# Reordering a slot on TensorE: the output product between the gate and the val matmuls

## The chip, the cores and the metric

The kernel runs on one core of one Trainium2 chip. The metric is the device time of one execution in microseconds. The input tensors lie in device memory as float32, and the output goes back as float32. The engines are named here as the profile names them: PE is TensorE's matmul, PEld its weight load, DVE is VectorE, ACT is ScalarE, POOL is GpSimd and SP is SyncE.

## The reference

Four batches of 6016 rows with 256 channels go through a cross-covariance attention, and the result goes through a gated feed-forward layer.

```python
def _attn_ref(q, k, v, tau):
    qn = q / (np.linalg.norm(q, axis=1, keepdims=True) + 1e-06)
    kn = k / (np.linalg.norm(k, axis=1, keepdims=True) + 1e-06)
    s = kn.transpose(0, 2, 1) @ qn / tau          # 256 x 256 per batch
    s = s - s.max(-1, keepdims=True)
    a = np.exp(s)
    a /= a.sum(-1, keepdims=True) + 1e-09
    return (v @ a).astype(np.float32)

def _moe_ref(x, w_gate, w_val, w_out):            # x: 24064 x 256, d_ff = 1536
    gate = 1.0 / (1.0 + np.exp(-(x @ w_gate)))
    val = x @ w_val
    return (gate * val @ w_out).astype(np.float32)
```

The scores `s` need a sum over all rows of a batch before that batch's feed-forward part can begin. The kernel folds the attention matrix into the weights: `G = a @ w_gate` and `H = a @ w_val`, so that `x @ w_gate` becomes `v @ G`. The sigmoid is written as a tanh: `sigmoid(z) * val` is half of `(tanh(z/2) + 1) * val`, and the half is carried by the constant 2 in the softmax's sums.

## The kernel before

The feed-forward part of batch `b` is cut into 12 chunks of 512 rows (the twelfth has 384), and each chunk into 12 **slots**, one for each block `f` of 128 of the 1536 hidden features. 4 x 12 x 12 makes 576 slots. A slot has these parts:

- **gate** and **val**: two matmuls of 512 columns each, into `ps_gate` and `ps_val`. Each of these PSUM pools has two buffers, so val of slot f needs the buffer that val of slot f-2 had.
- **tanh** on ACT, from `ps_gate` to `g_sb`.
- the **gating step** on DVE, `(tanh + 1) * val`, which writes block `f` of `hT` and frees `ps_val`.
- a **share of the output product** of the chunk before: 7 matmuls of 128 columns out of 84, into `ps_o`.
- **side work** for the next batch: scores on PE, squares on ACT, sums on DVE, additions and transfers on POOL.

```python
    psg = pool("psg", 2, space=PSUM)
    psv = pool("psv", 2, space=PSUM)
    pso = pool("pso", 2, space=PSUM)
    ...
    def glu(b, ci, f, between=None):
        ...
        ps_gate = psg.tile([P, CH], FP32, tag="g", name="ps_gate")
        ps_val = psv.tile([P, CH], FP32, tag="v", name="ps_val")
        for ps, w in ((ps_gate, G), (ps_val, H)):
            for ib in range(CB):                       # CB = 2
                mm(ps[:, :n], w[...][:, ib, ...], vT[:, ib, :nt, :], start=(ib == 0), stop=(ib == CB - 1))
            if between is not None and w is G:
                between()
        g_sb = gpool.tile([P, CH], FP32, tag="g", name="g_sb")
        nc.scalar.activation(out=g_sb[:, :n], in_=ps_gate[:, :n], func=ACT.Tanh, scale=0.5)
        nc.vector.scalar_tensor_tensor(
            out=hts[b, ci][:, f, :n], in0=g_sb[:, :n], scalar=1.0, in1=ps_val[:, :n],
            op0=ALU.add, op1=ALU.mult,
        )
```

The output product multiplies 2 x 2 blocks by a scheme with seven products in place of eight. Two of the seven (y1 and x1) take blocks of `hT` as they are; the other five (z1, x2, y2, z2, v2) take **sums** of two blocks, which DVE forms in `a_sum`. One `a_sum` forms one of the five sums for one half `g` of the hidden features. For half 0 this happens while the chunk itself is worked on, for half 1 in the first slots of the chunk after it.

```python
PRODUCTS = {  # name: (region of ps_o, left operand, right operand); a bare number is a sum
    "z1": (0, 1, 3), "y1": (1, (0, 0), 1), "x1": (2, (1, 1), 0), "x2": (2, 3, (0, 0)),
    "y2": (1, 2, (1, 1)), "z2": (0, 0, 2), "v2": (3, 4, 4),
}
ORDER = (
    (0, "y1"), (1, "y1"), (0, "x1"), (0, "z1"), (1, "x1"), (1, "z1"),
    (0, "x2"), (0, "y2"), (0, "z2"), (0, "v2"),
    (1, "x2"), (1, "y2"), (1, "z2"), (1, "v2"),
)
NEXT_SLOTS = {1: 1, 3: 3, 4: 2, 5: 0, 6: 4}        # slot: which sum, half 1, of the chunk before
OWN_SLOTS = {7: 1, 8: 3, 9: 2, 10: 0, 11: 4}       # slot: which sum, half 0, of this chunk
    ...
    def run_work(work, share):                         # take this share of the list, run it
        upto = sum(w[0] for w in work) * share
        done = 0
        while work and done < upto:
            cost, fn, *args = work.pop(0)
            fn(*args)
            done += cost
    ...
    for b in range(B):
        side = side_work(b)
        for ci in range(NCH):
            final = (b, ci) == (B - 1, NCH - 1)
            for f in range(FC):
                mid = gh_mid.get(f) if (b, ci) == (0, 0) else None
                glu(b, ci, f, None if mid is None else (lambda: gh_pieces(mid)))
                if prev is not None:
                    if f == 4:
                        store()
                    if f + final in NEXT_SLOTS and prev != (0, 0):
                        a_sum(*prev, 1, NEXT_SLOTS[f + final])
                    run_work(work, 1 / max(1, FC - final - f))
                if f in OWN_SLOTS and not final and (b, ci) != (0, 0):
                    a_sum(b, ci, 0, OWN_SLOTS[f])
                for fn, a in spill.get((b, ci, f), []) + side.get((ci, f), []):
                    fn(*a)
```

Every product runs over six indices `i`; `i` 0 to 2 uses half 0 of a sum and `i` 3 to 5 half 1. When the product z1 or v2 of a half of the rows ends, ACT copies a part of the bank (z1) or all of it (v2) out of `ps_o`, POOL adds the copies together, and SP stores the rows. A chunk of 384 rows has 42 of the small matmuls and 12 of 256 columns. All engines work through their instructions in the order of this program.

Of the kernel before, what the change touches and what calls it, by code (L numbers as in the profile page):

```python
# [9 lines left out]
FP32 = mybir.dt.float32  # L10
BF16 = mybir.dt.bfloat16
INT32 = mybir.dt.int32
ACT = mybir.ActivationFunctionType
# [40 lines left out]
def kernel(  # L54
# [20 lines left out]
    nc = tc.nc  # L75
    P = nc.NUM_PARTITIONS
# [9 lines left out]
    FC = DFF // P  # L86
# [3 lines left out]
    CH = TPC * P  # L90
# [11 lines left out]
    def pool(name, bufs, **kw):  # L102
        return ctx.enter_context(tc.tile_pool(name=name, bufs=bufs, **kw))
# [10 lines left out]
    gpool = pool("gpool", 3)  # L114
# [13 lines left out]
    def mm(out, lhsT, rhs, start, stop, **kw):  # L128
        nc.tensor.matmul(out, lhsT=lhsT, rhs=rhs, start=start, stop=stop, **kw)  # L129
# [74 lines left out]
    for f0, nf in pieces:  # L204
        if f0 + nf == DFF:
            load_v(0, 1)
        for w, src in enumerate((moe_w_gate, moe_w_val)):
            nc.gpsimd.dma_start(
                out=w_sb[w][f0 // FG][:, :, ds(f0 % FG, nf)],
                in_=src.rearrange("(t p) f -> p t f", p=P)[:, :, ds(f0, nf)],  # L210
# [5 lines left out]
    for n in range(FC // TPC):  # L216
        w_f32[n] = f32pool.tile([P, TPC, C], FP32, tag="f32", name="w_f32")
        nc.gpsimd.dma_start(
            out=w_f32[n], in_=moe_w_out.rearrange("(t p) c -> p t c", p=P)[:, n * TPC : (n + 1) * TPC, :]
# [413 lines left out]
    def gh(b, piece, pl, tag, act=None):  # L633
        gh_store(b, piece, gh_mms(b, piece, pl, tag), piece[3] == 0 if act is None else act)
# [25 lines left out]
    def glu(b, ci, f, between=None):  # L660
        t0, nt = groups[ci]
        n = nt * P
        G, H = st[b]["gh"]
        vT = vts[b, ci]
        if f == 0:
            hts[b, ci] = hpool.tile([P, FC, CH], BF16, tag="hT", name="hT")
        ps_gate = psg.tile([P, CH], FP32, tag="g", name="ps_gate")
        ps_val = psv.tile([P, CH], FP32, tag="v", name="ps_val")
        for ps, w in ((ps_gate, G), (ps_val, H)):
            for ib in range(CB):  # L670
                mm(
                    ps[:, :n],
                    w[f // (FG // P)][:, ib, ds(f % (FG // P) * P, P)],
                    vT[:, ib, :nt, :],
                    start=(ib == 0),
                    stop=(ib == CB - 1),
                )
            if between is not None and w is G:
                between()
        g_sb = gpool.tile([P, CH], FP32, tag="g", name="g_sb")  # L680
        nc.scalar.activation(out=g_sb[:, :n], in_=ps_gate[:, :n], func=ACT.Tanh, scale=0.5)  # L681
        nc.vector.scalar_tensor_tensor(  # L682
            out=hts[b, ci][:, f, :n],
            in0=g_sb[:, :n],
            scalar=1.0,
            in1=ps_val[:, :n],
            op0=ALU.add,
            op1=ALU.mult,
        )
# [3 lines left out]
    def a_sum(b, ci, g, m):  # L693

        nt = groups[ci][1]
        half = nt // 2
        hT = hts[b, ci]
        if (b, ci, g) not in sums:
            sums[b, ci, g] = spool.tile(
                [P, len(A_SUMS), FC // 4, CH // 2], BF16, tag=f"s{g}", name="sums", bufs=2 - g  # L700
            )
        (r0, k0), op, (r1, k1) = A_SUMS[m]
        f0, f1 = g * (FC // 2), (g + 1) * (FC // 2)
        nc.vector.tensor_tensor(  # L704
            out=sums[b, ci, g][:, m, :, : half * P],
            in0=hT[:, f0 + k0 : f1 : 2, ds(r0 * half * P, half * P)],
            in1=hT[:, f0 + k1 : f1 : 2, ds(r1 * half * P, half * P)],
            op=op,
        )
# [94 lines left out]
    def run_work(work, share):  # L804
# [8 lines that stand above are left out]
    def store():  # L813
        while stores:
            b, ci = stores.pop(0)
            t0, nt = groups[ci]
            nc.sync.dma_start(out=out_rows[b][:, t0 : t0 + nt, :], in_=ffn.pop((b, ci))[:, :nt, :])
# [43 lines left out]
    for g, (t0, nt) in enumerate(groups0):  # L861
# [11 lines left out]
        while adds:  # L873
            w, last_sq = adds.pop()
# [157 lines left out]
    def gh_pieces(ns):  # L1032
        for n in ns:
            gh(0, gh_first[n], *gh_banks[n % 4])

    prev = None
# [3 lines that stand above are left out]
            final = (b, ci) == (B - 1, NCH - 1)  # L1040
            for f in range(FC):
                mid = gh_mid.get(f) if (b, ci) == (0, 0) else None
                glu(b, ci, f, None if mid is None else (lambda: gh_pieces(mid)))
                if prev is not None:
                    if f == 4:
                        store()
                    if f + final in NEXT_SLOTS and prev != (0, 0):
                        a_sum(*prev, 1, NEXT_SLOTS[f + final])
                    run_work(work, 1 / max(1, FC - final - f))
                if f in OWN_SLOTS and not final and (b, ci) != (0, 0):  # L1050
                    a_sum(b, ci, 0, OWN_SLOTS[f])
                for fn, a in spill.get((b, ci, f), []) + side.get((ci, f), []):
                    fn(*a)
                if (b, ci) == (0, 0):
                    gh_pieces(gh_end.get(f, ()))
            prev = (b, ci)
            if not final:
                work = out_work(*prev)
# [39 lines left out]
```

## Time and profile before

| What | Value |
|---|---|
| median of 3 runs | 803.82 us (802.44 to 803.94) |
| span of the profiled execution | 799.6 us |
| granted TensorE clock, mean | 0.998 |
| PE busy | 779.7 us, 6875 matmuls |
| PEld busy | 497.6 us |
| DVE busy | 713.9 us |
| ACT busy | 525.6 us |
| POOL busy | 398.9 us |
| 576 gating steps on DVE | 385.3 us busy, 670 ns each on average |
| 576 tanh on ACT | 337.9 us busy, 589 ns each on average |
| 460 `a_sum` on DVE | 283.4 us busy, 616 ns each on average |

The page gives, for each engine, the time in which at least one of its instructions was under way. Rows of the costliest groups read: line, engine, operation, written tile <- read tiles, shape, count, then busy time and mean duration, then the idle time of that engine just before these instructions and what ended most of it. The timeline gives start, duration and the instruction. Matmuls overlap: one of 512 columns is shown with 0.38 us, but the next one starts 0.216 us after it. So the distance from start to start tells PE's rate.

### The profile page before, as it was taken

To read this page: it belongs to the slowest core of one execution; us is meant where nothing else is said; L and a number is where in the kernel's file an instruction comes from. 1 tells how busy PE (TensorE), PEld (TensorE's weight loads), DVE (VectorE), ACT (ScalarE), POOL (GpSimd) and SP (SyncE) were. 2 spreads that over 40 slices of the span, in tenths; PEclk is the share of its full clock that TensorE was granted. 3 is DMA by queue.
4 is the path that set the end of the run, shared out by engine and by line. 5 is a ranking of instruction groups with operands and counts; after the bars stand their busy time and mean duration, and the time that the engine had idled before them with its cause. 6 is when DMAs were issued, how large, how long until landed. Compare 5 with 4: busy or idle time off the path is not lost.

```text
span 799.6 us, 18217 instructions
## 1 busy us (share of the span) xinstructions
PE 779.7 (98%) x6875; PEld 497.6 (62%) x6875; DVE 713.9 (89%) x1228; ACT 525.6 (66%) x891; POOL 398.9 (50%) x618
## 2 busy tenths in 40 slices
PE   3899999999999999999999999999999999999998
PEld 2556666666666666666666666666666566666666
DVE  5768999999979999999988999999998898998996
ACT  3666777766667767676667777666666565665664
POOL 3564545446453566565743565565744244444433
PEclk9999999999999999999999999999999999999999
DMA  9997758432777899862577699977234323423302
GB/s 214 198 199 133 131 96 139 93 67 54 135 143 140 170 174 200 171 114 54 115 137 146 132 163 186 174 147 139 56 66 84 67 56 80 74 60 72 82 27 74
DMA packets 82776, 95.16 MB, mean 119 GB/s; under 512 B 52512, under 2 KB 58528, under 8 KB 82688
## 3 DMA queue, kind: packets, MB, share of 16 engines
q0 software_dynamic: 25616, 55.85, 39.5%
q1 hardware_dynamic: 56496, 37.30, 21.2%
q8 instruction: 53, 0.87, 0.4%
q10 hardware_dynamic: 576, 0.85, 0.3%
q14 instruction: 35, 0.29, 0.1%
HBM read 79.04 MB, written 24.64 MB: 130 GB/s over the span
## 4 chain that ended last, share of the span: by engine, by line
PE 94%; DMA 4%; DVE 1%; issue 0%; ACT 0%; POOL 0%; DVEq 0%; POOLq 0%
PE ps_gate L129 30%; PE ps_val L129 30%; PE ps_o L129 27%; DMA qk_sb<-in_k_dram 4%; PE ps_s L129 4%; PE ps_gh L129 3%; DVE hT L682 0%; DVE sums L704 0%; DVE qs L364 0%; PE ps_end L129 0%; PE ps_n L129 0%; DVE x_sb L543 0%; PE ps_r L129 0%; ACT e_sb L561 0%; POOL qk_sb L148 0%
## 5 line engine op out<-in xcount | busy, mean ns | idle before, releaser
L681 ACT ACTIVATE g_sb<-ps_gate 128x512 f32<-128x512 f32 (+1 forms) x576 | 337.9, 589 | 224.7 <-PE ps_gate L129 212.3
L682 DVE SCALAR_TENSOR_TENSOR hT<-g_sb,ps_val 128x512 bf16<-128x512 f32 (+1 forms) x576 | 385.3, 670 | 67.1 <-ACT g_sb L681 52.3
L129 PE MATMUL ps_val<-vT,gh_H 128*128 128x512 bf16 (+1 forms) x1152 | 337.5, 375 | 0.5 <-DVE hT L682 0.5
L129 PE MATMUL ps_gate<-vT,gh_G 128*128 128x512 bf16 (+1 forms) x1152 | 337.6, 375 | 0.0
L704 DVE TENSOR_TENSOR sums<-hT 128x768 bf16<-128x768 bf16 (+1 forms) x460 | 283.4, 616 | 0.0
L129 PEld LDWEIGHTS <-sums 128*128 128x128 bf16 x2670 | 182.9, 98 | 82.2 <-DVE sums L704 0.4
L129 PEld LDWEIGHTS <-gh_H 128*128 128x128 bf16 x1152 | 112.7, 98 | 131.5 <-issue 1.2
L775 POOL TENSOR_TENSOR out_sb<-out_sb,m_sb 128x256 f32<-128x256 f32 x89 | 78.8, 885 | 186.1 <-ACT out_sb L765 163.0
L129 PE MATMUL ps_o<-w_sums,sums 128*128 128x128 bf16 x1602 | 154.4, 219 | 0.0
L129 PEld LDWEIGHTS <-hT 128*128 128x128 bf16 x1200 | 88.3, 98 | 46.8
L759 POOL TENSOR_TENSOR m_sb<-m_sb 128x128 f32<-128x128 f32 x89 | 44.9, 504 | 127.1 <-ACT m_sb L758 126.7
L129 PEld LDWEIGHTS <-gh_G 128*128 128x128 bf16 x1152 | 92.5, 98 | 12.2 <-DVE gh_G L629 0.3
L129 PE MATMUL ps_o<-w_out_sb,sums 128*128 128x128 bf16 x1068 | 96.2, 219 | 0.0
L129 PE MATMUL ps_o<-w_sums,hT 128*128 128x128 bf16 x1068 | 95.5, 219 | 0.0
L776 POOL TENSOR_TENSOR out_sb<-out_sb 128x256 f32<-128x256 f32 x89 | 76.6, 861 | 7.0
L760 POOL TENSOR_TENSOR m_sb<-m_sb 128x128 f32<-128x128 f32 x89 | 56.6, 636 | 7.0
L765 ACT COPY out_sb<-ps_o 128x512 f32<-128x512 f32 x89 | 52.2, 586 | 11.4 <-PE ps_o L129 8.9
L129 PE MATMUL ps_s<-qk_sb 128*128 128x256 bf16 (+1 forms) x194 | 34.1, 292 | 15.7 <-DMA qk_sb<-in_k_dram 8.6
L758 ACT COPY m_sb<-ps_o 128x384 f32<-128x384 f32 x89 | 42.6, 479 | 3.7 <-PE ps_o L129 1.1
L257 ACT ACTIVATE sq<-qk_sb 128x1024 bf16<-128x1024 bf16 (+3 forms) x36 | 35.6, 1009 | 12.0 <-DMA qk_sb<-in_k_dram 11.9
L297 ACT ACTIVATE sq<-qk_sb 128x1024 bf16<-128x1024 bf16 (+1 forms) x40 | 41.2, 1031 | 0.0
L129 PEld LDWEIGHTS <-qk_sb 128*128 128x128 bf16 x286 | 26.7, 102 | 21.7 <-issue 10.9
(102 smaller groups left out, 448.0 us busy)
## 6 DMA issues: line engine op xcount, KB each, us to landing
out_dram<-out_sb SPq DMA_DIRECT2D x43, 512.0 KB, 3.4
v_sb<-in_v_dram POOLq DMA_DIRECT2D x44, 256.0 KB, 5.4
acc<-sq POOLq DMA_DIRECT2D x16, 512.0 KB, 7.0
qk_sb<-in_q_dram POOLq DMA_DIRECT2D x14, 512.0 KB, 10.3
qk_sb<-in_k_dram POOLq DMA_DIRECT2D x14, 512.0 KB, 8.2
qs<-qk_sb POOLq DMA_DIRECT2D x20, 256.0 KB, 5.5
qk_sb<-in_q_dram POOLq DMA_DIRECT2D x15, 256.0 KB, 4.6
qk_sb<-in_k_dram POOLq DMA_DIRECT2D x15, 256.0 KB, 5.6
```

The costliest lines, as they stand in the source:

```text
L129: nc.tensor.matmul(out, lhsT=lhsT, rhs=rhs, start=start, stop=stop, **kw)
L257: nc.scalar.activation(out=sq[:, :nt, :], in_=src[:, :nt, :], func=ACT.Square)
L297: nc.scalar.activation(out=s["sq", w][:, u0 : u0 + n, :], in_=src[:, u0 : u0 + n, :], func=ACT.Square)
L681: nc.scalar.activation(out=g_sb[:, :n], in_=ps_gate[:, :n], func=ACT.Tanh, scale=0.5)
L682: nc.vector.scalar_tensor_tensor(out=hts[b, ci][:, f, :n], in0=g_sb[:, :n], scalar=1.0, in1=ps_val[:, :n], op0=ALU.add, op1=ALU.mult,)
L704: nc.vector.tensor_tensor(out=sums[b, ci, g][:, m, :, : half * P], in0=hT[:, f0 + k0 : f1 : 2, ds(r0 * half * P, half * P)], in1=hT[:, f0 ...
L758: nc.scalar.copy(m, states[p]["ps"][:, : 3 * P].rearrange("p (n c) -> p n c", c=P))
L759: nc.gpsimd.tensor_tensor(out=m[:, 1, :], in0=m[:, 1, :], in1=m[:, 2, :], op=ALU.add)
L760: nc.gpsimd.tensor_tensor(out=m[:, 2, :], in0=m[:, 1, :], in1=m[:, 0, :], op=ALU.add)
L765: nc.scalar.copy(o[:, p : p + half + 1 : half, :], states[p]["ps"].rearrange("p (t c) -> p t c", c=C),)
L775: add(out=ends, in0=ends, in1=states[p]["m"][:, 1:3, :], op=ALU.add)
L776: add(out=ends, in0=ends, in1=mids, op=ALU.subtract)
```

## The change: where the output product stands in a slot

The change moves each slot's share of the output product from behind val to between gate and val. `glu` has a hook for this, `between`, which the first chunk already used for other matmuls. The tanh is now issued right after the gate matmuls, ahead of the hook, so that in ACT's order it stays ahead of the copies of `ps_o` that the output product may call for. The aim is that tanh runs while PE is at the output product, so that it is done by the time val is.

```diff
         ps_gate = psg.tile([P, CH], FP32, tag="g", name="ps_gate")
         ps_val = psv.tile([P, CH], FP32, tag="v", name="ps_val")
+        g_sb = gpool.tile([P, CH], FP32, tag="g", name="g_sb")
         for ps, w in ((ps_gate, G), (ps_val, H)):
             for ib in range(CB):
                 mm(
@@
-            if between is not None and w is G:
-                between()
-        g_sb = gpool.tile([P, CH], FP32, tag="g", name="g_sb")
-        nc.scalar.activation(out=g_sb[:, :n], in_=ps_gate[:, :n], func=ACT.Tanh, scale=0.5)
+            if w is G:
+                nc.scalar.activation(out=g_sb[:, :n], in_=ps_gate[:, :n], func=ACT.Tanh, scale=0.5)
+                if between is not None:
+                    between()
         nc.vector.scalar_tensor_tensor(
@@
                 mid = gh_mid.get(f) if (b, ci) == (0, 0) else None
-                glu(b, ci, f, None if mid is None else (lambda: gh_pieces(mid)))
+                if prev is not None:
+                    mid = lambda: run_work(work, 1 / max(1, FC - final - f))
+                elif mid is not None:
+                    mid = lambda ns=mid: gh_pieces(ns)
+                glu(b, ci, f, mid)
                 if prev is not None:
                     if f == 4:
                         store()
                     if f + final in NEXT_SLOTS and prev != (0, 0):
                         a_sum(*prev, 1, NEXT_SLOTS[f + final])
-                    run_work(work, 1 / max(1, FC - final - f))
```

No instruction is added or taken away. In a slot PE had gate, val, output, scores; it now has gate, output, val, scores. DVE's order is as before: gating step, `a_sum`, side work. In ACT's order only the first chunk differs, where tanh now stands ahead of the copies that build G and H.

## The prediction

> **What bounds the kernel now.** I began with the page's busy times and its chain of waits.
>
> ```profile
> PE 779.7 (98%) x6875; PEld 497.6 (62%) x6875; DVE 713.9 (89%) x1228; ACT 525.6 (66%) x891; POOL 398.9 (50%) x618
> PE 94%; DMA 4%; DVE 1%; issue 0%; ACT 0%; POOL 0%; DVEq 0%; POOLq 0%
> ```
>
> PE holds 94% of the chain that ended last, and the 4% of DMA is the head, where the first q and k arrive. DVE is second and close. A busy share of 98% doesn't prove that PE runs at its rate, so I went on to the timeline of PE in a middle slot.
>
> ```profile
> 495.78 0.59 PE L129 MATMUL ps_gate<-vT,gh_G 128*128 128x512 bf16 x2
> 496.21 0.59 PE L129 MATMUL ps_val<-vT,gh_H 128*128 128x512 bf16 x2
> 496.64 0.55 PE L129 MATMUL ps_o<-w_sums,sums 128*128 128x128 bf16 x7
> 497.03 0.28 PE L129 MATMUL ps_s<-qs,qk_sb 128*128 128x128 bf16 x2
> 497.14 0.59 PE L129 MATMUL ps_gate<-vT,gh_G 128*128 128x512 bf16 x2
> ```
>
> From start to start, gate takes 0.43 us, val 0.43, seven output matmuls 0.39, two scores 0.11: 1.36 us together. That is 4 x 0.216 + 9 x 0.056. I took the same distances over the whole trace: the medians are 216 ns behind a matmul of 512 columns and 56 ns behind one of 128. After 60 us, the distances that exceed their kind's value by over 60 ns add up to only **1.1 us** of excess: 0.78 us ahead of two val groups, 0.25 us ahead of one score and 0.09 us elsewhere. So PE runs back to back for 740 us. It waits for nobody.
>
> Then the waits, and the two costliest groups:
>
> ```profile
> DVE hT L682 <- ACT g_sb L681: 52.3, 117, 1.3
> PE ps_val L129 <- DVE hT L682: 0.5, 2, 0.3
> PEld L129 <- DVE sums L704: 0.4, 1, 0.4
> L681 ACT ACTIVATE g_sb<-ps_gate 128x512 f32<-128x512 f32 (+1 forms) x576 | 337.9, 589 | 224.7 <-PE ps_gate L129 212.3
> L682 DVE SCALAR_TENSOR_TENSOR hT<-g_sb,ps_val 128x512 bf16<-128x512 f32 (+1 forms) x576 | 385.3, 670 | 67.1 <-ACT g_sb L681 52.3
> ```
>
> The 52.3 us in which DVE waits for tanh are what the change aims at. But that is idle time of an engine that isn't the bound. PE's own waits for DVE, the second and third line, come to 0.9 us.
>
> [...] this trace shows 56 in such streams[...], and output matmuls have no slack from weight loads that another order could win back. [...] loads of sums begin about 0.2 us ahead of their matmuls. So a late sum holds up all that PE has behind it, val included. [...] The `a_sum` rows fit that: 550 ns in the median, 1809 ns at most, with POOL additions beside the long ones. The rows don't prove the cause.
>
> **The change, part by part.**
>
> *Removed:* nothing on PE. The same 6875 matmuls are issued at the same rate. What can vanish is PE's wait ahead of val for its PSUM buffer, 0.78 us. Val comes 0.39 us later in its slot (7 x 56 ns), while the gating step that frees its buffer moves by at most about 0.25 us (next paragraph), so this wait gets more room. The most that can be won is the whole 1.1 us, **0.1%**.
>
> *Moved, DVE:* before, the gating step could start 1.26 us after the slot's gate at the earliest (minimum over the trace, 1.39 in the median): 0.43 for gate, about 0.2 until tanh starts, 0.6 tanh. After, tanh is done at that same 1.23 to 1.26, but val ends its issue at 0.43 + 0.39 + 0.43 = 1.25, and with the same 0.2 us of latency the step starts at 1.45 to 1.46. So steps that used to start before 1.46 come later, by 0.2 us at most; later ones, where DVE was behind, don't move. Over all steps of 512 columns the mean move is 0.09 us. DVE's wait for tanh turns into a wait for val of about the same length. It doesn't become shorter: DVE's work and PE's period stay as they are.
>
> *Moved, the output product:* relative to its slot's gate it stands **0.43 us earlier** (val's two matmuls), while the sums come no earlier and in part up to 0.2 us later. This is the cost. From the order of the program I paired each of the 3822 output matmuls in the loop with the sum or gating step that it needs, and took the room between that operation's end and the matmul's start. The median is over 8 us. The tight ones are all the first use of half 1 of a sum, `i` = 3: z1 in slot 3 (or slot 2 for 384 rows), y2, z2 and v2 in slots 6 to 8. For chunks of 512 rows, z1 has 1.01 us in the median and 0.06 at the least. One is already late, at 475 us:
>
> ```profile
> 473.53 1.42 DVE L704 TENSOR_TENSOR sums<-hT 128x768 bf16<-128x768 bf16 x1
> 474.48 0.59 PE L129 MATMUL ps_val<-vT,gh_H 128*128 128x512 bf16 x2
> 474.99 0.17 PEld L129 LDWEIGHTS <-sums 128*128 128x128 bf16 x3 [0.42 <-DVE sums L704]
> 475.00 0.34 PE L129 MATMUL ps_o<-w_sums,sums 128*128 128x128 bf16 x3
> ```
>
> The sum ended at 474.95, and val had filled the time up to 474.91. With the output product ahead of val, PE would stand still from 474.48 to 474.99. That one slot costs 0.4 to 0.5 us.
>
> *The sum:* a matmul that had to wait still shows 0.06 us of room, so a slot becomes late where its smallest room is under 0.43 + 0.06 = 0.49 us. Within a chunk I count only the largest shortfall, because PE's delay gives room to the next slots too. That makes **13 chunks and 2.4 us**. With the full extra delay of the gating step (a threshold of 0.65) it is 18 chunks and 4.9 us; with 0.55 it is 14 and 3.3. Tight slots are mostly those in which DVE was behind, whose sums don't move, so I stay near the low end: +2.5 us. Less the 0.8 us ahead of val this is **+1.7 us**, and 803.8 + 1.7 = **805.5 us**.
>
> *Off the path:* ACT's copies of `ps_o` are asked for 0.43 us sooner relative to gate. Before, a copy at a slot's end delayed the next tanh; after, it ends while val runs. A tanh that starts late because of a square (1.05 us) has 0.82 us of output and val to hide in. POOL's additions follow the copies, and their waits (163.0 us behind the copies in one row of the page) are idle time of a half-empty engine. In the first chunk tanh goes ahead of the copies that build G and H, with a few tenths of a microsecond either way.
>
> **The rivals.**
>
> *Tanh was the hidden bound, so the change wins several per cent.* For it: 52.3 us of DVE waits for tanh, and DVE busy 89%, 92% between 60 and 780 us (662.66 of 720). Against it: DVE's lateness reaches PE in only about 1 us of 740. Were it true, PE's starts would show gaps; they don't. It would make 765 to 785 us. I hold it for all but excluded.
>
> *PE becomes bound to DVE's sums in most chunks.* For it: the median room of the z1 sum is only 1.01 us, and up to 0.63 of that goes; DVE has only 8% of spare time, so a backlog drains slowly. Were every one of 46 product chunks to lose 0.4 us, that is +18 us, and 822 us. Against it: nine tenths of the z1 rooms are over 0.72 us, still enough after the shift.
>
> *Nothing happens at all.* The rooms shift with how POOL and DVE happen to meet, and a wait of PE gives DVE time to catch up, so the late slots could cost under 1 us and cancel what val no longer waits. It would make 803 to 804.
>
> **Range and chances.** The runs of before spread over 1.5 us. The lower end is no late sum, no wait ahead of val and a low draw: 802.5. The upper end is twice the larger estimate of the late sums, 2 x 2.4 to 4.9 us, less a little: 809.5. A 2% gain needs 787.7 us, which is below what 6875 matmuls at their rate permit: 0.5%. A 2% loss needs 819.9 us, almost the second rival in full: 2.5%. Between lies 97%.
>
> **What would show it.** In the profile after: PE busy and matmul count nearly unchanged; DVE's wait for tanh small, and in its place a wait of the gating step for val, some tens of microseconds; PE's wait for val's buffer gone; weight loads waiting for DVE's sums up from 0.4 to 2 to 5 us in ten to twenty places, most in slots 2, 3 and 6 to 8. The step about the sums is wrong if these loads wait for under 1 us or over 10 us. The whole prediction is wrong if the distances between matmul starts change by themselves when blocks of 128 and 512 columns alternate in another order, or if DVE's operations become longer because they meet POOL's at other times.

## The result, and the profile after

The changed kernel takes 809.46 us in the median of 6 runs (805.96 to 811.84), against 803.13 us (801.15 to 803.94) for the kernel before in the same measurement. The ratio is **1.0081, with a 95% interval of 1.0053 to 1.0108**: slower by about 6.5 us. The profiled execution was the shortest of the six, with a span of 804.2 us.

The page of the changed kernel, busy times and chain:

```profile
PE 781.5 (97%) x6861; PEld 497.0 (62%) x6875; DVE 705.0 (88%) x1228; ACT 513.8 (64%) x891; POOL 396.8 (49%) x618
PE 89%; DVE 5%; DMA 4%; issue 1%; ACT 0%; POOL 0%; DVEq 0%; ACTq 0%; POOLq 0%
```

DVE is busy for less time than before (705.0 us against 713.9), and yet it now holds 5% of the chain, where it had 1%. (14 matmul records are missing from this trace, and 14 or 17 from seven others of this study; I left out the distances across them.) The waits say what the chain means. The columns are engine, line, what was waited for, total us, times, longest:

```profile
DVE hT L683 <- PE ps_val L129: 50.9, 131, 0.8
DVE hT L683 <- ACT g_sb L680: 10.5, 23, 1.0
PEld L129 <- DVE sums L705: 8.9, 21, 0.9
PE ps_o L129 <- DVE sums L705: 2.1, 7, 0.4
```

The change does what it is for: DVE's wait for tanh falls from 52.3 to 10.5 us. But 50.9 us of waiting for val take its place, as the gating step (L683 here) can't start before val. And PE's weight loads wait 8.9 us for sums, in 21 places, where it was 0.4 us in one.

Here is one such place in the timeline of the changed kernel, slot 2 behind a chunk of 384 rows:

```profile
233.13 0.59 PE L129 MATMUL ps_gate<-vT,gh_G 128*128 128x512 bf16 x2
233.14 0.69 DVE L683 SCALAR_TENSOR_TENSOR hT<-g_sb,ps_val 128x512 bf16<-128x512 f32 x1
233.56 0.33 PE L129 MATMUL ps_o<-w_sums,sums 128*128 128x128 bf16 x3
233.75 0.35 DVE L705 TENSOR_TENSOR sums<-hT 128x384 bf16<-128x384 bf16 x1
234.15 0.34 PE L129 MATMUL ps_o<-w_sums,sums 128*128 128x128 bf16 x3 [0.26 <-DVE sums L705]
234.33 0.59 PE L129 MATMUL ps_val<-vT,gh_H 128*128 128x512 bf16 x2
```

Three output matmuls run at once. The other three need the sum that starts at 233.75 and ends at 234.10, and val, which the program has behind them, started at 234.33. The fourth matmul would have started at 233.56 + 3 x 0.056 = 233.73; it started at 234.15. PE lost 0.42 us.

To count all such losses I used the measure of the prediction: the excess of each distance between matmul starts over its kind's value, where it is over 60 ns, after 60 us. I sorted it by what the late matmul belongs to. The table holds every run of this study; spans and waits are those of the profiled execution, ratios those of all runs.

| Kernel | ratio to before (95%) | span, us | excess, us | output matmuls | val | other |
|---|---|---|---|---|---|---|
| before | 1 | 799.6 | 1.1 | 0.1 | 0.8 | 0.3 |
| the change, first | 1.0081 (1.0053 to 1.0108) | 804.2 | 5.5 | 5.0 | 0.1 | 0.5 |
| the change, again | 1.0084 (1.0070 to 1.0097) | 806.0 | 7.5 | 5.5 | 2.0 | 0 |
| sums one slot sooner | 1.0057 (1.0044 to 1.0070) | 803.1 | 4.1 | 0 | 3.8 | 0.3 |
| hook in loose slots only | 1.0055 (1.0042 to 1.0068) | 802.3 | 4.1 | 0.5 | 3.0 | 0.6 |
| hook in tight slots only | 1.0074 (1.0060 to 1.0088) | 804.2 | 5.4 | 3.1 | 2.1 | 0.2 |
| share ahead of gate | 1.0564 (1.0547 to 1.0581) | 843.5 | 43.3 | 41.0 | 2.3 | 0 |
| half-1 sums not used | 1.0022 (1.0014 to 1.0029) | 800.6 | 2.5 | 0 | 2.2 | 0.3 |
| share one slot late | 0.9997 (0.9988 to 1.0005) | 799.8 | 0.2 | 0 | 0 | 0.2 |
| before, sums sooner | 1.0016 (1.0009 to 1.0024) | 800.9 | 2.6 | 0 | 2.3 | 0.2 |
| three of seven matmuls | 1.0019 (1.0010 to 1.0028) | 801.4 | 3.2 | 3.1 | 0.1 | 0 |
| change, no output additions | 1.0083 (1.0065 to 1.0100) | 806.8 | 7.7 | 6.6 | 0 | 1.1 |
| before, no output additions | 1.0028 (1.0017 to 1.0039) | 802.3 | 3.3 | 3.3 | 0 | 0 |
| change, no folds | 1.0057 (1.0037 to 1.0077) | 803.1 | 4.4 | 2.5 | 1.5 | 0.4 |
| change, quiet POOL | 1.0010 (1.0000 to 1.0020) | 800.9 | 2.4 | 1.6 | 0 | 0.8 |
| before, quiet POOL | 0.9993 (0.9981 to 1.0005) | 798.6 | 0 | 0 | 0 | 0 |
| sum ahead of gating step | 1.0000 (0.9990 to 1.0011) | 799.4 | 1.1 | 0 | 1.1 | 0 |

For most rows the excess grows with the span nearly one for one (5.5 - 1.1 = 4.4 us against 804.2 - 799.6 = 4.6 for the change). So the loss is PE standing still, in most places for DVE, and not a slower PE. The profiled execution of the change was its shortest, so its 4.6 us are less than the 6.5 of the medians; the longer executions have no trace.

### The profile page after: what moved, and what is told of

It is laid out like the page before. It is cut to its first block, busy times and chain, and to the rows that moved or that the text cites. A ratio compares the mean times of both kernels' runs of the same rounds, so it can differ in the third digit from the quotient of the medians.

```text
span 804.2 us, 18203 instructions
## 1 busy us (share of the span) xinstructions
PE 781.5 (97%) x6861; PEld 497.0 (62%) x6875; DVE 705.0 (88%) x1228; ACT 513.8 (64%) x891; POOL 396.8 (49%) x618
## 4 chain that ended last, share of the span: by engine, by line
PE 89%; DVE 5%; DMA 4%; issue 1%; ACT 0%; POOL 0%; DVEq 0%; ACTq 0%; POOLq 0%
PE ps_val L129 29%; PE ps_gate L129 28%; PE ps_o L129 26%; DMA qk_sb<-in_k_dram 4%; PE ps_s L129 3%; PE ps_gh L129 2%; DVE hT L683 2%; DVE sums L705 1%; DVE acc L315 1%; DVE qs L364 0%; PE ps_end L129 0%; ACT m_sb L759 0%; ACT g_sb L680 0%; DVE x_sb L543 0%; PE ps_n L129 0%
## 5 line engine op out<-in xcount | busy, mean ns | idle before, releaser
L683 DVE SCALAR_TENSOR_TENSOR hT<-g_sb,ps_val 128x512 bf16<-128x512 f32 (+1 forms) x576 | 386.5, 672 | 80.1 <-PE ps_val L129 50.9
L705 DVE TENSOR_TENSOR sums<-hT 128x768 bf16<-128x768 bf16 (+1 forms) x460 | 267.7, 582 | 0.0
L776 POOL TENSOR_TENSOR out_sb<-out_sb,m_sb 128x256 f32<-128x256 f32 x89 | 69.4, 780 | 184.0 <-ACT out_sb L766 159.5
L129 PE MATMUL ps_o<-w_sums,sums 128*128 128x128 bf16 x1602 | 156.1, 219 | 2.4 <-DVE sums L705 2.1
L129 PEld LDWEIGHTS <-gh_G 128*128 128x128 bf16 x1152 | 104.2, 98 | 82.2 <-DVE gh_G L629 0.3
L760 POOL TENSOR_TENSOR m_sb<-m_sb 128x128 f32<-128x128 f32 x89 | 43.5, 489 | 136.3 <-ACT m_sb L759 136.2
L129 PEld LDWEIGHTS <-gh_H 128*128 128x128 bf16 x1152 | 90.1, 98 | 3.3 <-DVE gh_H L629 0.3
L777 POOL TENSOR_TENSOR out_sb<-out_sb 128x256 f32<-128x256 f32 x89 | 80.7, 907 | 7.0
L761 POOL TENSOR_TENSOR m_sb<-m_sb 128x128 f32<-128x128 f32 x89 | 61.6, 692 | 7.0
L129 PEld LDWEIGHTS <-qk_sb 128*128 128x128 bf16 x286 | 29.5, 103 | 43.4 <-issue 9.9
```

The source lines that it names most:

```text
L683: nc.vector.scalar_tensor_tensor(out=hts[b, ci][:, f, :n], in0=g_sb[:, :n], scalar=1.0, in1=ps_val[:, :n], op0=ALU.add, op1=ALU.mult,)
L705: nc.vector.tensor_tensor(out=sums[b, ci, g][:, m, :, : half * P], in0=hT[:, f0 + k0 : f1 : 2, ds(r0 * half * P, half * P)], in1=hT[:, f0 ...
L760: nc.gpsimd.tensor_tensor(out=m[:, 1, :], in0=m[:, 1, :], in1=m[:, 2, :], op=ALU.add)
L761: nc.gpsimd.tensor_tensor(out=m[:, 2, :], in0=m[:, 1, :], in1=m[:, 0, :], op=ALU.add)
L776: add(out=ends, in0=ends, in1=states[p]["m"][:, 1:3, :], op=ALU.add)
L777: add(out=ends, in0=ends, in1=mids, op=ALU.subtract)
```

## The experiments

**First four: where does PE wait?** Theory A was that of the prediction, the half-1 sums; B and C were a slower PE cadence and longer DVE operations. The change once more, unaltered:

> The changed kernel once more, unaltered, for a second profile. Theory A (PE waits for the half-1 sums in slots 2, 3, 6, 7 and 8, because the output product stands 0.43 us earlier): the ratio is again 1.005 to 1.011, and the excess in the distances between matmul starts, 5.5 us in the first profile (1.1 us in the kernel before), is larger where the span is longer, about 10 us at a span of 809. Theory B (PE's own cadence is worse when blocks of 512 and 128 columns alternate in this order): the medians of 216 and 56 ns shift, and the waits don't explain the span. Theory C (DVE and POOL operations get longer because they meet at other times): DVE's busy time is above the 713.9 us of before.

807.73 us against 801.26. Distances between matmul starts are again 216 and 56 ns in the median, and DVE's busy time is no higher (707.8 us against 713.9): B falls, and C falls as far as DVE's total goes. The output matmuls' waits are much as in the first profile, but 2.0 us of waits ahead of val are new. So one execution of the same program has waits that another doesn't have.

The half-1 sums sooner:

```diff
-NEXT_SLOTS = {1: 1, 3: 3, 4: 2, 5: 0, 6: 4}
+NEXT_SLOTS = {0: 1, 2: 3, 3: 2, 4: 0, 5: 4}
@@
-                    if f + final in NEXT_SLOTS and prev != (0, 0):
-                        a_sum(*prev, 1, NEXT_SLOTS[f + final])
+                    if f in NEXT_SLOTS and prev != (0, 0):
+                        a_sum(*prev, 1, NEXT_SLOTS[f])
```

> The changed kernel with every half-1 sum formed one slot sooner (slots 0, 2, 3, 4, 5 in place of 1, 3, 4, 5, 6); PE's order stays gate, output, val. Theory A: the sums gain about one slot, 1.3 us, of room, which is over the 0.43 to 0.63 us lost, so PE's waits for sums fall under 0.5 us and the time comes back to that of before, 801.5 to 803.5. Theory B or C: the loss stays, 808 to 811.

805.75 us. Theory A had the wait right and the time wrong: the waits for sums are gone, from 5.0 to 0, but only a third of the loss is. The waits of the sums_early profile:

```profile
PE ps_val L129 <- DVE hT L683: 2.5, 4, 0.9
```

PE now stops ahead of val, whose PSUM buffer the gating step frees. One wait had turned into another on the same engine.

The hook in part of the slots only (the second kernel with `f in (2, 3, 6, 7, 8)`):

```diff
+                inside = f not in (2, 3, 6, 7, 8)
                 if prev is not None:
-                    mid = lambda: run_work(work, 1 / max(1, FC - final - f))
+                    mid = (lambda: run_work(work, 1 / max(1, FC - final - f))) if inside else None
@@
+                    if not inside:
+                        run_work(work, 1 / max(1, FC - final - f))
```

> The output product stands between gate and val only in the seven slots 0, 1, 4, 5, 9, 10 and 11, where no half-1 sum is used for the first time; in slots 2, 3, 6, 7 and 8 it stays behind val as before. Theory A: the waits are gone but for those that before had, 802.5 to 804.5. Theory B: seven twelfths of the loss of 6.5 us remain, about 807. Theory C: likewise something between, 805 to 808.

> The complement: the output product stands between gate and val only in slots 2, 3, 6, 7 and 8, and behind val in the other seven. Theory A: nearly the whole loss is there, 807.5 to 810.5. Theory B: five twelfths of it, about 806. The time that this kernel and the one with the loose slots lose against before should add up to the loss of the full change if the slots act independently.

805.80 and 806.30 us: both expectations of A failed. The two losses, 4.5 and 5.0 us, add up to more than the 6.5 of the whole change. The loose kernel has a cost of its own that I hadn't seen: where a slot without the hook stands two after a slot with it, its val comes 0.39 us sooner after that slot's val than in either pure order, and that takes from the room that its buffer has. Most of its waits stand there, ahead of val in slots 2 and 7. So mixing the orders doesn't split the effect cleanly.

**Next four: earlier output, or later gating step?** The rival, theory D, was that the later gating step makes the loss. The share ahead of its gate, in the kernel before:

```diff
+                if prev is not None:
+                    run_work(work, 1 / max(1, FC - final - f))
                 glu(b, ci, f, None if mid is None else (lambda: gh_pieces(mid)))
@@
-                    run_work(work, 1 / max(1, FC - final - f))
```

> The kernel before with each slot's share of the output product moved ahead of its gate: output, gate, val. The output product comes 0.86 us earlier than in the kernel before, tanh and the gating step stay where they were relative to val. Theory A (what costs is that the output product comes too early for the half-1 sums): by the rooms in the trace of before, a shift of 0.86 us is too much in 40 of the 46 product chunks, 12 us by the largest shortfall of each and 20 us by all slots, so 811 to 820 against 801.3. Theory D (what costs is the later gating step, whose lateness DVE carries on into its bursts): the gating step isn't later here, so under 3 us, 801.5 to 804.

846.12 us. The shift in this text is wrong: relative to the gate the share moves from behind gate and val (+0.86) to ahead of gate by its own length (-0.39), 1.25 us in all. At that shift plus the 0.06 of a wait the rooms of before (a room is the time between the end of a sum and the start of the matmul that needs it) give 29 us by the largest shortfall of each chunk and 84 us by all slots; 43 us of excess were measured. The waits of this kernel:

```profile
PEld L129 <- DVE sums L704: 47.5, 106, 1.1
DVE hT L682 <- ACT g_sb L681: 101.7, 239, 1.3
```

With tanh and the gating step unmoved, an earlier output product alone costs a great deal. D alone doesn't hold.

No use of the half-1 sums, and the share one slot late:

```diff
-                lhsT = sums[b, ci, g][:, a, j, ds(p * P, P)]
+                lhsT = sums[b, ci, g][:, a, j, ds(p * P, P)] if g == 0 else hT[:, 2 * i, ds(p * P, P)]
```

> The changed kernel, in which the products take a block of hT itself wherever they took a half-1 sum; DVE still forms all sums, and nothing reads those of half 1. Left out is the use of these sums, so the output is not the reference's. No wait for a half-1 sum is possible, and every engine's order is that of the change. Theory A alone: 801 to 802.5. Theory D: PE runs into the other thing that it needs of DVE, the freed ps_val, so 3 to 4 us of waits ahead of val stay, 804 to 806, as with the sums one slot sooner.

```diff
                 if prev is not None:
-                    mid = lambda: run_work(work, 1 / max(1, FC - final - f))
+                    mid = None if f == 0 else (lambda: run_work(work, 1 / max(1, FC - final - f + 1)))
@@
+                    if f == FC - 1 - final:
+                        run_work(work, 1)
```

> The changed kernel with the share of the slot before between gate and val: PE alternates gate, output, val as in the change, but each output matmul comes 0.43 us later than in the kernel before instead of 0.43 us earlier. The gating step is as late as in the change; the copies of ps_o and POOL's additions move by 0.43 us in the same direction as the gating step. Theory A: no wait for sums, 801 to 802.5. Theory D: the waits ahead of val stay, 804 to 806. Theory E (the waits ahead of val come from DVE operations and POOL additions that meet, and the change moved the two apart by 0.7 us): here they stand as in the kernel before to within 0.2 us, so 801.5 to 803.

The first took 803.29 us: without any wait for these sums the loss is 1.5 to 1.8 us, nearly all of it ahead of val, about half of what D expected. The second took 801.38 us against 801.79, no loss at all. (Its share comes 0.82 us later than before relative to gate, not 0.43 as the text has it, by the same slip.) PE alternates as in the change, and the gating step starts as late: 0.27 us after the end of val's issue in the median, as in the change. So **the order gate, output, val costs nothing by itself, nor does the later gating step by itself**, as long as the sums have this room.

The sums in the new slots, but in the kernel before:

> The kernel before, with its order gate, val, output, and the half-1 sums formed in slots 0, 2, 3, 4, 5: the control for the run that did the same to the changed kernel and still lost 4.5 us. If that loss belongs to the changed order, this one stays at 801 to 802. If it comes from the sums standing in slots 0 and 2, where other DVE work of a burst is, this one loses 2 to 4 us as well.

802.71 us, 1.3 us slower than the kernel before by the ratio, ahead of val. If the two add up, which the loose and tight slots didn't, about 1.3 of the 4.5 us that stayed with sums one slot sooner came from that edit's own crowding of DVE.

**Next four: how the two shifts meet, and POOL.** Only three of the seven matmuls between gate and val:

```diff
-                    mid = lambda: run_work(work, 1 / max(1, FC - final - f))
+                    mid = lambda: run_work(work, 3 / 7 / max(1, FC - final - f))
@@
+                    run_work(work, 4 / 7 / (max(1, FC - final - f) - 3 / 7))
```

> The changed kernel with only the first three of a slot's seven output matmuls between gate and val, and four behind val. Then val ends 0.17 us later in its slot, not 0.39, and the gating step can start no later than tanh lets it, as in the kernel before; but the first uses of half-1 sums of z1 (first of slot 3), z2 (third of slot 7) and v2 (second of slot 8) are among the three and come 0.43 us earlier as in the change. Theory A (the output product's earlier place): by the rooms of before some 3 us of waits for sums, 803.5 to 805.5. Theory D (the later gating step makes most of the loss): under 1 us, 801 to 802.5.

803.23 us, between the two expectations and just under that of A. The excess is 3.1 us on output matmuls. The gating step starts as in the kernel before (1.35 us after gate in the median, against 1.39). So the output product's earlier place, without a later gating step, costs about 1.5 us of time, for three of the five sums: the first half-1 uses of x2 and y2 stay behind val here. The full change costs 6.5. The rest isn't the gating step alone (share one slot late): both shifts take from the same room. How much of it belongs to x2 and y2 was not separated.

Without POOL's four output additions, and the control:

```diff
-            nc.gpsimd.tensor_tensor(out=m[:, 1, :], in0=m[:, 1, :], in1=m[:, 2, :], op=ALU.add)
-            nc.gpsimd.tensor_tensor(out=m[:, 2, :], in0=m[:, 1, :], in1=m[:, 0, :], op=ALU.add)
@@
-            add(out=ends, in0=ends, in1=states[p]["m"][:, 1:3, :], op=ALU.add)
-            add(out=ends, in0=ends, in1=mids, op=ALU.subtract)
```

> The changed kernel without POOL's four additions per half of an output chunk (89 times four, 240 us of POOL); ACT's copies and the stores stay. Left out are the additions that join the seven products, so the output is not the reference's. Theory E (the worst backlogs of DVE come from operations that met one of these additions, and the change moved where they meet): the waits ahead of val vanish and the waits for sums shrink to those that follow from the order alone, about 1.3 us in slot 2 behind the short chunks and up to 1 us in the chunks with the folds; 801.5 to 803.5. If DVE's backlog comes from its own bursts: still 805 to 808.

> The kernel before without the same additions, as the control. All theories: the 1.1 us of PE's waits go, nothing else, 800 to 801.5; the ratio to before is 0.998 to 1.000. The difference to the changed kernel without the additions is what the change costs where DVE and POOL don't meet: by theory E 1 to 3 us, else 5 to 7.

808.59 and 804.18 us: both too slow, the control too. The timeline of the control shows why:

```profile
381.37 0.88 POOL L435 TENSOR_TENSOR x_sb<-sm_sb 128x128 f32<-128x128 f32 x2
381.84 3.28 DVE L704 TENSOR_TENSOR sums<-hT 128x768 bf16<-128x768 bf16 x1
382.20 1.68 POOL L435 TENSOR_TENSOR x_sb<-x_sb,sm_sb 128x128 f32<-128x128 f32 x4
383.85 0.85 POOL L435 TENSOR_TENSOR x_sb<-sm_sb 128x128 f32<-128x128 f32 x2
385.18 0.34 PE L129 MATMUL ps_o<-w_out_sb,sums 128*128 128x128 bf16 x3 [1.51 <-DVE sums L704]
```

A sum that takes 0.55 us elsewhere took 3.28 us, until the row of eight additions on POOL was over, and PE stood for 1.67 us. In the kernel before, POOL was still at output additions then, and the same eight came 1.7 us later and met the sums otherwise. The pair couldn't answer the question, but apart from these two stops per kernel (and the half clock described at the end) the change had 1.9 us of excess and the control none.

The folds left out:

```diff
-        for n in steps:
-            nc.vector.tensor_tensor(out=acc[:, :n, :], in0=acc[:, :n, :], in1=acc[:, n : 2 * n, :], op=ALU.add)
+        for n in steps[:0]:
+            pass
```

> The changed kernel without the folds of the squares' sums on DVE, some 4 us of DVE's work per batch around the turn from the eighth to the ninth chunk; the norms are formed from one block of rows, so the output is not the reference's. The first two profiles of the change show about 0.9 us of waits in each of the two ninth chunks with long folds. If DVE's own bursts make the waits there: these 1.8 us go and the rest stays, 805.5 to 806.5. If the waits there come from the order alone: no change, 807.5 to 808.5.

805.73 us, in the range for DVE's own bursts. The waits in the ninth chunks are gone, and a meeting with POOL elsewhere (1.5 us ahead of one val) took the place of part of them.

**Last three: the quiet pair and a way out.** The output additions left out as above, and one copy on ACT in place of the eight:

```diff
-        tt(o[0][0], z1, z2, ALU.add)
-        ...                                  # eight additions on POOL in all
-        tt(o[1][0], x1, x2, ALU.add)
+        nc.scalar.copy(s["s"].rearrange("p i (h c) -> p (i h) c", c=P), s["m"][:, :4, :])
```

> The changed kernel without POOL's output additions and with one copy on ACT in place of POOL's eight additions on the score blocks[...]. Left out are these additions, so the output is not the reference's. Theory E (DVE's large delays come from meeting POOL additions): the waits for sums that follow from the order alone stay, 1.9 us as in the pair before without its two long stops, and no wait ahead of val; 802 to 803 where the kernel before without the additions has 800 to 801. If DVE's own load makes the waits: 5 us or more over that control.

> The control for the last: the kernel before with the same additions left out. All theories: no PE wait over 60 ns after the head, and 800 to 801, which is also the floor that PE's rate sets. The difference to the changed kernel is what the change costs where DVE doesn't meet POOL's additions: 1.5 to 2.5 us by theory E, over 4 us otherwise.

802.58 and 800.62 us: **2.0 us** of difference. The control has no excess at all after 60 us, so I take its 800.62 us for what PE's rate permits, an estimate. DVE's sums take 538 ns on average in both, where the kernel before has 616 and the change 582, so these additions do lengthen sums:

```profile
L704 DVE TENSOR_TENSOR sums<-hT 128x768 bf16<-128x768 bf16 (+1 forms) x460 | 283.4, 616 | 0.0
L705 DVE TENSOR_TENSOR sums<-hT 128x768 bf16<-128x768 bf16 (+1 forms) x460 | 267.7, 582 | 0.0
L695 DVE TENSOR_TENSOR sums<-hT 128x768 bf16<-128x768 bf16 (+1 forms) x460 | 247.5, 538 | 0.0
L694 DVE TENSOR_TENSOR sums<-hT 128x768 bf16<-128x768 bf16 (+1 forms) x460 | 247.6, 538 | 0.0
```

(The pages of before, of the change, of the change with quiet POOL and of before with quiet POOL.) So of the 6.5 us, about 2.0 are there without POOL's additions, and about 4.5 only with them. In the ninth chunks the quiet kernel still loses 0.16 us each, where the change loses 0.89: the folds make the waits there together with POOL's additions.

Not all of the 2.0 us are waits for sums. Of the quiet change's 2.4 us of excess, 0.8 stands ahead of one gate, in the timeline of that kernel:

```profile
498.27 1.06 ACT L297 ACTIVATE sq<-qk_sb 128x1024 bf16<-128x1024 bf16 x1 [2.03 <-DMA acc<-sq]
499.23 1.07 ACT L670 ACTIVATE g_sb<-ps_gate 128x512 f32<-128x512 f32 x2
499.86 0.59 PE L129 MATMUL ps_gate<-vT,gh_G 128*128 128x512 bf16 x2 [0.65 <-ACT g_sb L670]
```

A square on ACT had waited for a transfer, tanh was late behind it, and gate waited for the buffer that tanh frees. That is a wait for ACT, and one trace can't tell how often it comes.

Each sum ahead of its slot's gating step, in the changed kernel:

```diff
-                    mid = lambda: run_work(work, 1 / max(1, FC - final - f))
+                    def mid():
+                        if f + final in NEXT_SLOTS and prev != (0, 0):
+                            a_sum(*prev, 1, NEXT_SLOTS[f + final])
+                        if f in OWN_SLOTS and not final:
+                            a_sum(b, ci, 0, OWN_SLOTS[f])
+                        run_work(work, 1 / max(1, FC - final - f))
```

(The two calls behind the gating step go.)

> The changed kernel with each sum issued ahead of its slot's gating step instead of behind it, in both halves. In the changed kernel DVE stands idle ahead of most gating steps until val is there; a sum of 0.55 us fits into that time, and each sum is ready some 0.7 us sooner. PE's order is that of the change. Combined theory (the output product's earlier place and the later gating step take from the same room of the half-1 sums, and the cost rises faster than their total): the waits for sums vanish, the waits ahead of val stay at 0 to 2 us, so 801 to 803.5 against 801.7. If the wait for val sets DVE's pace and a sum ahead of it delays the gating step: the waits ahead of val grow to several us, 805 or more.

801.90 us against 801.77, a ratio of 1.0000: the loss is gone, with PE's order left as it is in the change. No wait of PE for sums is left; 1.1 us of excess ahead of val are, of which the waits show 0.6:

```profile
PE ps_val L129 <- DVE hT L683: 0.6, 2, 0.4
```

It brings nothing over the kernel before, as PE's rate leaves about 1 us to win (an estimate: 801.77 less 800.62). No version here beats both kernels.

## Why the prediction was wrong

**The bound and the direction were right.** PE sets the time, and its matmuls keep their 216 and 56 ns. DVE's wait for tanh turned into one for val (50.9 us), the small buffer wait ahead of val went in the first profile, and the first half-1 products became late in slots 2, 3, 6, 7 and 8. The first rival, a gain of several per cent, is excluded as said.

**The size was too small by a factor of nearly four**: +1.7 us predicted, about +6.5 measured. The step that failed is *The sum*: its term for late sums, +2.5 us, measured 5.0 and 5.5 us at the output matmuls of the two profiles, and the 0.8 us to be won ahead of val came back as a loss of 2.0 us in the second. The weight loads waited for sums for 8.9 us in 21 places, where 2 to 5 us in ten to twenty were named. Three things in it were wrong.

*"Tight slots are mostly those in which DVE was behind, whose sums don't move, so I stay near the low end."* They do move. I took the room of the first half-1 use again in the profile after, over all five sums for the first half of a chunk's rows: the median fell from 1.00 to 0.43 us and the lower quartile from 0.88 to 0.26. That is a shift of 0.57 to 0.62 us where I had used 0.43. The gating step's later start reaches the tight sums too. It is also longer than I reckoned: I gave DVE the 0.2 us that ACT takes from the end of a matmul's issue to its start, but the gating step starts 0.27 us after the end of val's issue at the least, in the median too. So it starts 1.53 us after gate in the median, not 1.46, where before it was 1.39; the mean moved by 0.19 us, not by 0.09. The 0.43 of the output product and these 0.14 make the 0.57. The cost rises faster than the shift: 43 us at 1.25 (share ahead of gate), 5.0 at about 0.6, 3.1 at 0.43 with the gating step unmoved (three of seven matmuls, and so three of the five sums).

*"Within a chunk I count only the largest shortfall, because PE's delay gives room to the next slots too."* In the two ninth chunks with long folds, slot 3 lost 0.54 us and slot 7 another 0.35. A PE stop delays the next val and with it the next gating step, which is how I read that DVE gained so little. Counting all slots, with the output product's 0.43, the 0.09 that I had for the gating step and the 0.06 of a wait, the rooms of before yield 26 slots and 5.6 us; the two profiles show 5.0 and 5.5. This count was made afterwards, and its closeness is partly luck: with the 0.14 that the gating step moved in the median it gives 28 slots and 7.0 us. The places are no luck: of the 18 late output matmuls in the first profile, 15 stand in the 26 slots, with 4.7 of the 5.0 us, and 15 of the 22 in the second, with 4.8 of the 5.5. So the trace of before held the places and about the size. The slot that the prediction picked out, at 475 us and 0.4 to 0.5 us, lost 0.11 us in one profile and 0.38 in the other.

*What the last sentence of the prediction named and the sum left out:* DVE and POOL meeting at other times. This explains little of the late output matmuls, as the rooms of before already hold what POOL's additions took from DVE there. It shows in the waits ahead of val. Here is the same DVE operation, at the same turn of a chunk. In the timeline of before:

```profile
279.70 0.68 DVE L359 TENSOR_TENSOR qs<-qk_sb 128x1024 bf16<-128x1024 bf16 x1
280.84 1.04 POOL L775 TENSOR_TENSOR out_sb<-out_sb,m_sb 128x256 f32<-128x256 f32 x1
```

And in the second profile of the change:

```profile
280.92 1.75 DVE L359 TENSOR_TENSOR qs<-qk_sb 128x1024 bf16<-128x1024 bf16 x1
281.07 1.04 POOL L776 TENSOR_TENSOR out_sb<-out_sb,m_sb 128x256 f32<-128x256 f32 x1
282.60 1.27 DVE L683 SCALAR_TENSOR_TENSOR hT<-g_sb,ps_val 128x512 bf16<-128x512 f32 x2
283.32 0.59 PE L129 MATMUL ps_val<-vT,gh_H 128*128 128x512 bf16 x2 [0.57 <-DVE hT L683]
```

Before, POOL began 0.46 us after DVE's operation had ended. In the second profile DVE is 0.50 us later relative to its slot's gate and POOL 0.48 us sooner: POOL begins 0.15 us into the operation, which then takes 1.07 us longer, about the length of the addition, 1.04 us. By the starts shown DVE was first, by 0.15 us, and DVE's operation is the one that grew; what made it grow is not shown. The gating step behind it is late, and val waits. In the first profile of the change DVE was as late, but the same addition began 1.17 us after gate, against 1.09 before and 0.61 in the second, and the operation took 0.68 us. So the later DVE comes with the change, but where POOL falls differs between executions of the same program. Such meetings aren't more frequent (23 and 26 DVE operations over 300 ns above the median of their kind, where before had 57), but they meet a DVE with less room. I called POOL's waits "idle time of a half-empty engine" and looked no further.

That the quiet pair's 2.0 us lies near the predicted 1.7 is no proof of the sum, which was made from rooms that POOL's additions had shortened; and 0.8 us of its excess is a wait for ACT, which the prediction's *Off the path* had held to be hidden. Three readings of the prediction were off as well: in the trace of before a load of sums begins 0.21 us ahead of its matmul in the median only where that stands behind a matmul of 512 columns (330 of 2670), and 0.05 us ahead elsewhere; z1's first half-1 use has 0.95 us of room in the median (1.01 is that of its three half-1 matmuls together); and the upper end of 809.5 isn't twice the larger estimate, which would give 803.8 + 9.8 - 0.8 = 812.8.

**Left open.** The share of waits ahead of val and ahead of output matmuls varies from profile to profile (0.1 and 2.0 us ahead of val in two), and I can't say what it was in each run without a trace. That about 4.5 us need POOL's additions is shown by the quiet pair as a whole; that they act by lengthening DVE's operations is read from single places in the traces, and no run moved one meeting alone.

## What to carry to other kernels

Idle time that a wait shows on an engine beside the bound is worth nothing until it reaches the bound; a reordering of the bound's own work can win no more than the gaps between its starts, here 1.1 us of 740. When work moves ahead, list every operand that it takes from another engine with its room, add up all shifts that take from that room (the consumer's earlier place and the producer's later start), and count every short slot. Where the producer's operations grow beside those of a third engine, as DVE's did beside POOL's (1.75 us where 0.68 is usual), the rooms of one trace are partly a draw, so leave more margin than one profile asks for, or reorder the producer so that it works in its own wait, as the sum ahead of the gating step did.

## What the runs showed of the hardware

A sum that takes 0.55 us elsewhere took 3.28 us while eight POOL additions ran in a row, in the kernel before without output additions. In the trace of before, 204 sums of 128x768 elements had no addition of POOL beside them, and each took 0.54 to 0.55 us. The other 226 had one: 0.63 us in the median, 1.81 at most, and 106 of them still under 0.60. What makes the long ones longer is not shown.

In the changed kernel without output additions PE stood for 2.37 us at the same place; 1.3 us after this stop's end the trace has a stretch of 3.41 us in which the granted clock was half. The timeline of that kernel has two gate matmuls shown with 1.06 us in it, where two otherwise take 0.59:

```profile
385.64 0.34 PE L129 MATMUL ps_o<-w_out_sb,sums 128*128 128x128 bf16 x3 [2.21 <-DVE sums L705]
386.30 0.59 PE L129 MATMUL ps_gate<-vT,gh_G 128*128 128x512 bf16 x2
388.16 1.06 PE L129 MATMUL ps_gate<-vT,gh_G 128*128 128x512 bf16 x2
582.27 0.34 PE L129 MATMUL ps_o<-w_out_sb,sums 128*128 128x128 bf16 x3 [2.21 <-DVE sums L705]
584.19 0.59 PE L129 MATMUL ps_gate<-vT,gh_G 128*128 128x512 bf16 x2
```

The slowed matmuls add 1.1 us of excess. Whether the stop brought the stretch is not shown: the second stop of 2.37 us, which ends at 582.27 us, has none behind it. In the control, with stops of 1.67 us, the clock stayed full behind them, and its mean was 0.998. In three of the first six runs of the change the mean clock was 0.996, where the profiled one had 0.998. The profile has one such stretch, at 21 us in the head; a second one would account for the difference (an estimate: half of 3.41 us in 810 is 0.002), but those runs have no trace.
